# One k double of batch 3 turned by a transposing DMA instead of TensorE, in a fused sliding-window attention and MLP kernel

## The chip, the cores and the metric

The kernel runs on one core of one Trainium2 chip. The metric is the device time of one execution in microseconds (us); of several runs the median is taken. A core has five engines with a queue of instructions each: TensorE (PE, matrix products and transposes, into PSUM), VectorE (DVE), ScalarE (ACT), GpSimd (POOL) and SyncE (SP). SP computes nothing here; it issues nearly all the loads and stores and all the transposing DMAs, in the order of the program. PEld is TensorE's loading of weights, which overlaps with its products. Each engine works through its queue in order and waits for the others on semaphores.

## The reference

Eight batches of attention (8 heads, 576 tokens, head size 64) with a bias that falls linearly with distance, over a window of 128 tokens; the heads are then put side by side and go through an MLP with a hard-swish.

```python
scores = scale * np.matmul(q, k.transpose(0, 1, 3, 2))
rel = pos[:, None] - pos[None, :]
slopes = 2.0 ** (-8.0 * (np.arange(H) + 1) / H)
mask = (rel >= 0) & (rel < 128)
scores = np.where(mask, scores - slopes[:, None, None] * np.abs(rel), -1e9)
attn = softmax(scores)
x = (attn @ v).transpose(0, 2, 1, 3).reshape(B * S, H * D)     # 4608 x 512
h = x @ w_in                                                    # 4608 x 2048
out = (h * np.clip(h + 3.0, 0.0, 6.0) / 6.0) @ w_out            # 4608 x 512
```

Inputs and output are float32; inside, the kernel computes its products in bfloat16.

## The kernel before

**Groups.** Attention goes by groups g = 0 to 31: g = 4 * batch + pair of heads. A group needs q and k of its two heads turned, with the head dimension on the partitions (tiles qTb and kTb, two of each, one per parity of the batch), and v as it lies (vbuf). `scores(g)` makes the score products (lines 365 and 373), `exp_diag` and `exp_off` the exponentials on ScalarE (389, 413, 418), each followed by a mask on GpSimd (406, 415, 421), `values` the products with v (434, 442) in two parts, query tiles 0 to 2 and then 3 and 4, each followed by a reciprocal and a multiplication on VectorE into the tile avs (452, 453). `back(g)` turns avs into x^T: for g >= 8, other than 10 and 11, by a transposing DMA on SP (476); for groups 10 and 11 by five TensorE transposes and a copy on ScalarE (483, 489).

**MLP.** The tokens go in nine blocks of 512. A block has 16 up units (`moe_up`: four products at line 502, an activation on ScalarE at 521, a combination on VectorE at 522) and 16 down units (`moe_down`: four products at 552; after every fourth a VectorE copy, 561, and a store on SP, 562). These units are filler for TensorE: `fill(n)` issues the next n of them. An up unit is issued only when `done` says that all groups of its tokens have their x^T.

**Order.** The whole order of work is written by hand (a manual schedule): what the program says first goes first into each engine's queue. From batch 2 on the order is that of `segment`, whose pass g issues: scores(g); a turn, in passes 8 to 11; filler; the exponentials of g, with filler and values(g - 1) between them; back(g - 1); `stage_next(g)`; filler. In pass 12 scores(13) are issued as well, with the scores of 12 at the pass's beginning.

**How q and k get turned.** From batch 4 on, and for q of batch 3, `stage_next` loads the tokens of a whole tensor (`load_tokens`, five loads of up to 128 tokens on SP, line 112), GpSimd casts them to bfloat16 in tbuf (`cast_tokens`, 195), and one transposing DMA of 20 blocks of 128 columns turns them (`xbar`, 200). k of batch 3 goes another way: it is loaded as two doubles (four heads each; `load_double`, 98), cast by GpSimd (`prepare_double`, 228, in passes 8 and 9), and turned on TensorE by `double`: five transposes into a PSUM tile (243), a ScalarE copy to kTb (245), then four more and a second copy. Both use the PSUM buffer of tag "av", of which there is one; `values` takes its result tiles from the same buffer. The first double of k of batch 3 is turned in pass 10, the second in pass 11. Its scores come in passes 12 to 15.

**Around it on SP.** In pass 8, `stage_next` issues nothing on SP. In pass 9 SP issues x^T of group 8, then the five loads of v of batch 3 (from the table LOADS), then the transposing DMA of q of batch 3, which waits for GpSimd's five casts. v of batch 3 is cast on GpSimd in pass 12 (188, 191).

Of the kernel before, what the change touches and what calls it, by code (L numbers as in the profile page):

```python
# [11 lines left out]
BF16 = mybir.dt.bfloat16  # L12
# [6 lines left out]
def kernel(  # L19
# [9 lines left out]
    nc = tc.nc  # L29
    B, H, S, D = q.shape  # L30
# [5 lines left out]
    NP = H // 2  # L36
    NQ = 5
# [3 lines left out]
    RP, RT = 64, 9  # L41
# [24 lines left out]
    prs = ctx.enter_context(tc.tile_pool(name="prs", bufs=2))  # L66
# [14 lines left out]
    qTb = [held.tile([128, NP, NQ, 128], BF16, name=f"qTb{i}") for i in range(2)]  # L81
    kTb = [held.tile([128, NP, NQ, 128], BF16, name=f"kTb{i}") for i in range(2)]
# [19 lines left out]
    def tokens(b, nm):  # L102
        if (b, nm) not in ld:
            i = 2 + b % 2 if b < 3 else (3, 1, 0, 2)[(3 * (b - 3) + "qkv".index(nm)) % 4]
            ld[b, nm] = ldbuf[i][:, 0:NQ * H * D].rearrange("p (j h d) -> p j h d", j=NQ, h=H)
        return ld[b, nm]

    def load_tokens(b, nm):
        t = tokens(b, nm)
        for j in range(NQ):  # L110
            n = min(128, S - j * 128)
            nc.sync.dma_start(out=t[:n, j, :, :],
                              in_=src_of[nm][b, :, ds(j * 128, n), :].rearrange("h p d -> p h d"))
# [70 lines left out]
    def cast_tokens(b, nm):  # L184
        s = ld[b, nm]
        if nm == "v":
            for lo in (0, 2):
                nc.gpsimd.tensor_copy(  # L188
                    out=vbuf[b % 2][:, lo:lo + 2, :, 0:D].rearrange("p j h d -> p (j h) d"),
                    in_=s[:, lo:lo + 2, :, :].rearrange("p j h d -> p (j h) d"))  # L190
            nc.gpsimd.tensor_copy(out=vbuf[b % 2][:LAST, 4, :, 0:D], in_=s[:LAST, 4, :, :])
            return
        for j in range(NQ):
            m = min(128, S - j * 128)
            nc.gpsimd.tensor_copy(out=tbuf[:m, :, j, :],  # L195
                                  in_=s[:m, j, :, :].rearrange("p (i e) d -> p i (e d)", e=2))

    def xbar(b, nm):
        dst = (qTb if nm == "q" else kTb)[b % 2]
        nc.sync.dma_start_transpose(out=dst.rearrange("p h j c -> p (h j) c"),  # L200
                                    in_=tbuf.rearrange("p h j c -> p (h j c)"))

    st = {}
# [20 lines left out]
    def prepare_double(b, dp, copies, nms="kq", early=None):  # L224
        for nm, copy in zip(nms, copies):
            pr = prs.tile([128, RT, 2 * D], BF16, tag=f"pr{nm}", name="pr2")
            for e in range(2):
                copy(out=pr[:, :, ts(e, D)],  # L228
                     in_=ldbuf["qk".index(nm)][:, ds((2 * dp + e) * RT * D, RT * D)].rearrange(
                         "p (t d) -> p t d", t=RT))  # L230
                if early and (nm, e) == (nms[0], 0):
                    early()
            st[b, dp, nm] = pr
# [3 lines left out]
    def double(b, dp, nm, part, tag, copy):  # L237
        src = st[b, dp, nm]
        t0, t1 = ((0, 5), (5, RT))[part]
        tp = BANKS[tag].tile([128, t1 - t0, 128], BF16, tag=tag, name="tp2",  # L240
                             padded_shape=[128, 8, 128])
        for t in range(t0, t1):
            nc.tensor.transpose(tp[:, t - t0, :], src[:, t, :], ident)  # L243
        dst = (qTb if nm == "q" else kTb)[b % 2][:, 2 * dp:2 * dp + 2, :, :]
        copy(out=dst.rearrange("p i j c -> p i (j c)")[:, :, 0:S].rearrange(  # L245
                 "p i (a t) -> p i a t", t=RT)[:, :, :, t0:t1],
             in_=tp.rearrange("p t (a i) -> p i a t", i=2))

    def wide_double(b, dp, nm, copy):
# [219 lines left out]
    def by_xbar(g):  # L469
        return g >= XB and g != XB + 2 and g != XB + 3  # L470
# [103 lines left out]
    def fill(n):  # L574
        for _ in range(n):
            if at[0] == len(units):
                return
            nt, fn, step = units[at[0]]
            if fn is moe_up and done[0] < NP * (min((nt * NT + NT - 1) // S, B - 1) + 1):
                return  # L580
            fn(nt if fn is moe_up else nt - 1, step)
            at[0] += 1

    V, P, A = nc.vector.tensor_copy, nc.gpsimd.tensor_copy, nc.scalar.copy

    LOADS = {9: "v3", 10: "q4", 12: "k4", 13: "v4", 14: "q5", 16: "k5", 17: "v5", 18: "q6",
             20: "k6", 21: "v6", 22: "q7", 24: "k7", 25: "v7"}

    VCAST = {15: 4, 19: 5, 23: 6, 27: 7}
# [1 line left out]
    def stage_next(g):  # L591
        b, hp = divmod(g, NP)
        nb = b + 1
        if g == 2 * NP:
            cast_tokens(2, "v")
        for n in LOADS.get(g, "").split():
            load_tokens(int(n[1]), n[0])
        if nb == 3 and hp < 2:
            prepare_double(3, hp, (P,), "k")
        if nb == 3 and hp == 1:  # L600
            cast_tokens(3, "q")
            xbar(3, "q")
        elif nb < B and nb > 3 and hp < 2:
            cast_tokens(nb, "qk"[hp])
            xbar(nb, "qk"[hp])
        if VCAST.get(g):
            cast_tokens(VCAST[g], "v")
# [110 lines left out]
    def segment(lo, hi, fills):  # L718
        for g in range(lo, hi + 1):
            f = fills(g)  # L720
            if by_xbar(g - 2):
                done[0] = g - 1
            if lo < g < hi and g != 3 * NP + 1:
                scores(g)
            turn = {2 * NP: (2, 1, "k"), 2 * NP + 1: (2, 1, "q"),
                    2 * NP + 2: (3, 0, "k"), 2 * NP + 3: (3, 1, "k")}.get(g)
            if turn:
                double(*turn, 0, "av", A)
            fill(f[0])
            if turn:  # L730
                double(*turn, 1, *(("h", V) if turn[0] == 2 else ("av", A)))
            if g < hi:
                exp_diag(g, 0)
            fill(f[1])
            if g < hi:
                exp_diag(g, 1)
            if g == 3 * NP:
                cast_tokens(3, "v")
            if g > lo:
                values(g - 1, (0, 1, 2))  # L740
            fill(f[2])
            if g < hi:
                exp_off(g, 0)
            fill(f[3])
            if g < hi:
                exp_off(g, 1)
            if g > lo:
                values(g - 1, (3, 4))
            fill(f[4])
            if g > lo and by_xbar(g - 1):  # L750
                back(g - 1)
            fill(f[5])
            if g < hi:
                stage_next(g)
            fill(1)
            if g == 3 * NP:
                scores(g + 1)
            if g > lo and not by_xbar(g - 1):
                back(g - 1)
                done[0] = g  # L760
            fill(f[6] - 1)
# [51 lines left out]
```

## Time and profile before

| | us |
|---|---|
| median of 3 runs | 321.58 |
| the runs | 321.58, 320.84, 323.06 |
| the profiled execution | 320.94 |
| its span, first to last instruction | 319.2 |
| PE busy | 310.1 |
| PEld busy | 164.9 |
| ACT busy | 195.7 |
| DVE busy | 173.1 |
| POOL busy | 141.2 |

The profile is of one execution. Its times are counted from the first instruction. Busy times are sums of an engine's instructions, with overlaps counted once; a PE that is shown busy need not be at its peak. The granted TensorE clock was 0.999 of full speed. A row of a timeline has the start, the length, the engine, the line of the kernel, the operation, what it writes <- what it reads, shapes, how many were merged, and in brackets an idle time before it and what ended it. A `q` behind an engine's name is its queue: a row that issues a DMA. The time from the issue of a DMA to its landing stands in the table of DMA issues.

### The profile page before, as it was taken

What the parts mean: (1) busy time and instruction counts of PE and PEld (TensorE: products, weight loads), DVE (VectorE), ACT (ScalarE), POOL (GpSimd) and SP (SyncE); (2) the same over time, 40 slices, a digit from 0 to 9 for tenths busy, and PEclk for the clock granted to TensorE, in tenths of its full rate; (3) what the DMA queues carried; (4) which work ended last, traced back from release to release, by engine and by line L of the source; (5) the groups of instructions that cost most, each with busy time, mean ns of one, the idle gap of its engine ahead of it and who ended that gap; (6) DMA issues with size and microseconds to landing.
All of it is one profiled execution on the core that took longest, in us unless ns stands there. A gap on an engine that the chain in (4) does not pass through costs nothing.

```text
span 319.2 us, 7124 instructions
## 1 busy us (share of the span) xinstructions
PE 310.1 (97%) x2775; PEld 164.9 (52%) x2775; DVE 173.1 (54%) x338; ACT 195.7 (61%) x334; POOL 141.2 (44%) x249
## 2 busy tenths in 40 slices
PE   7879999999999999999999999999999999999996
PEld 5565465455545454445677654444444444444443
DVE  6667675554355655655565556555656455455510
ACT  4748976877767776676676667666764344244401
POOL 8464493684496477266744673663331000000000
PEclk9999999999999999999999999999999999999999
DMA  7999999999999999998999999962212110000112
GB/s 281 199 323 225 256 260 195 249 231 194 215 252 157 239 208 211 205 222 194 207 205 211 209 190 196 225 93 68 38 39 88 53 36 33 33 33 35 66 56 75
DMA packets 131425, 51.90 MB, mean 163 GB/s; under 512 B 118976, under 2 KB 123328, under 8 KB 131392
## 3 DMA queue, kind: packets, MB, share of 16 engines
q1 hardware_dynamic: 126160, 45.36, 68.0%
q0 software_dynamic: 4224, 4.19, 8.2%
q10 hardware_dynamic: 1008, 1.90, 1.6%
q8 instruction: 21, 0.34, 0.5%
q14 instruction: 12, 0.10, 0.1%
HBM read 36.70 MB, written 9.44 MB: 145 GB/s over the span
## 4 chain that ended last, share of the span: by engine, by line
PE 86%; DMA 5%; ACT 4%; POOL 2%; DVE 2%; issue 1%; POOLq 0%
PE ops L552 38%; PE hps L502 36%; DMA w_in_sb<-in_moe_w_in_dram 3%; PE sce L365 3%; PE av L442 2%; PE av L434 2%; DMA ldbuf<-in_k_dram 2%; ACT r L521 2%; PE ops L533 1%; ACT kTb L245 1%; ACT gbuf L399 1%; PE tp L243 1%; DVE gbuf L522 0%; ACT gbuf L377 0%; PE tb L483 0%
## 5 line engine op out<-in xcount | busy, mean ns | idle before, releaser
L522 DVE SCALAR_TENSOR_TENSOR gbuf<-r,hps 128x512 bf16<-128x512 f32 x144 | 98.7, 688 | 101.0 <-ACT r L521 99.8
L521 ACT ACTIVATE r<-hps,bias 128x512 f32<-128x512 f32 x144 | 98.9, 689 | 86.8 <-PE hps L502 86.6
L502 PE MATMUL hps<-xT,w_in_sb 128*128 128x512 bf16 (+1 forms) x640 | 144.9, 358 | 0.6 <-ACT xT L489 0.3
L552 PE MATMUL ops<-w_out_sb,gbuf 128*128 128x512 bf16 x560 | 137.8, 379 | 0.0
L502 PEld LDWEIGHTS <-w_in_sb 128*128 128x128 bf16 x640 | 59.3, 98 | 55.0 <-issue 0.8
L552 PEld LDWEIGHTS <-gbuf 128*128 128x128 bf16 x560 | 51.9, 98 | 56.3
L415 POOL TENSOR_SCALAR_AFFINE_SELECT po<-po 128x512 bf16<-128x512 bf16 x48 | 30.3, 636 | 32.5 <-ACT po L413 32.4
L406 POOL TENSOR_SCALAR_AFFINE_SELECT pd<-pd 128x512 bf16<-128x512 bf16 x48 | 29.8, 634 | 33.5 <-ACT pd L389 33.5
L389 ACT ACTIVATE pd<-sce,bias_d 128x512 bf16<-128x512 f32 x48 | 31.7, 684 | 5.4 <-PE sce L373 2.7
L561 DVE COPY osb<-ops 128x512 f32<-128x512 f32 x33 | 22.7, 688 | 20.0 <-PE ops L552 17.5
L195 POOL CAST tbuf<-ldbuf 128x512 bf16<-128x512 f32 (+1 forms) x45 | 25.6, 614 | 16.8 <-issue 9.3
L413 ACT ACTIVATE po<-sce,bias_o 128x512 bf16<-128x512 f32 x48 | 33.0, 687 | 0.0
L453 DVE TENSOR_TENSOR avs<-av,rc 128x384 bf16<-128x384 f32 (+1 forms) x48 | 23.6, 491 | 1.6
L442 PEld LDWEIGHTS <-pd 128*128 128x128 bf16 x192 | 14.3, 97 | 8.3 <-issue 0.5
L434 PE MATMUL av<-vbuf,po 128*128 128x65 bf16 x192 | 18.0, 193 | 0.0
L442 PE MATMUL av<-vbuf,pd 128*128 128x65 bf16 x192 | 17.3, 193 | 0.3 <-ACT kTb L245 0.3
L434 PEld LDWEIGHTS <-po 128*128 128x128 bf16 x192 | 14.3, 98 | 2.9 <-DVE avs L453 0.5
L188 POOL CAST vbuf<-ldbuf 128x1024 bf16<-128x1024 f32 x14 | 14.2, 1043 | 3.5 <-DMA ldbuf<-in_v_dram 3.5
L418 ACT ACTIVATE p4buf<-sce,bias_d 128x64 bf16<-128x64 f32 x48 | 15.5, 323 | 0.0
L228 POOL CAST pr<-ldbuf 128x576 bf16<-128x576 f32 x20 | 12.9, 670 | 5.1 <-DMA ldbuf<-in_k_dram 3.1
L365 PE MATMUL sce<-qTb,kTb 64*64 64x192 bf16 (+1 forms) x368 | 11.9, 245 | 0.0
L365 PEld LDWEIGHTS <-kTb 64*64 64x64 bf16 x368 | 7.1, 106 | 8.6 <-issue 8.5
(104 smaller groups left out, 208.4 us busy)
## 6 DMA issues: line engine op xcount, KB each, us to landing
out_dram<-osb SPq DMA_DIRECT2D x33, 256.0 KB, 2.5
ldbuf<-in_v_dram SPq DMA_DIRECT2D x32, 256.0 KB, 5.2
ldbuf<-in_q_dram SPq DMA_DIRECT2D x20, 256.0 KB, 5.3
ldbuf<-in_k_dram SPq DMA_DIRECT2D x16, 256.0 KB, 4.4
ldbuf<-in_q_dram SPq DMA_DIRECT2D x12, 288.0 KB, 7.0
ldbuf<-in_k_dram SPq DMA_DIRECT2D x12, 288.0 KB, 6.3
w_in_sb<-in_moe_w_in_dram POOLq DMA_DIRECT2D x4, 512.0 KB, 9.2
w_out_sb<-in_moe_w_out_dram POOLq DMA_DIRECT2D x4, 512.0 KB, 10.3
```

The lines of the kernel that those rows point to most:

```text
L195: nc.gpsimd.tensor_copy(out=tbuf[:m, :, j, :], in_=s[:m, j, :, :].rearrange("p (i e) d -> p i (e d)", e=2))
L365: nc.tensor.matmul(sce[e][lo:lo + 64, j, :, :].rearrange("p s c -> p (s c)")[:, ds(lo, n)], lhsT=kT[r, j, lo:lo + 64], rhs=qT[r, ds(128 * ...
L389: nc.scalar.activation(out=pd[:, e, :, :], in_=st["sce"][e][:, :, 0, :], func=ACT.Exp, bias=bias_d[:, h:h + 1], scale=scale)
L406: nc.gpsimd.affine_select(out=pd[:, e, :, :], in_=pd[:, e, :, :], pattern=[[0, 4], [1, 128]], channel_multiplier=-1, base=0, compare_op=AL ...
L413: nc.scalar.activation(out=po[:, e, :, :], in_=sc[:, :, 1, :], func=ACT.Exp, bias=bias_o[:, h:h + 1], scale=scale)
L415: nc.gpsimd.affine_select(out=po[:, e, :, :], in_=po[:, e, :, :], pattern=[[0, 4], [-1, 128]], channel_multiplier=1, base=-1, compare_op=A ...
L434: nc.tensor.matmul(out_av, lhsT=po[:, e, qt % 4 if full(g) else qt - 1, :], rhs=vb[:, qt - 1, h, :], start=True, stop=False)
L442: nc.tensor.matmul(out_av, lhsT=d, rhs=vb[:, qt, h, :], start=(qt == 0), stop=True)
L502: nc.tensor.matmul(hps[:, lo:hi], lhsT=w_in_sb[:, ks, ts(ms, 128)], rhs=xT[:, ks, ds(src, hi - lo)], start=(ks == 0), stop=(ks == n_ks - 1))
L521: nc.scalar.activation(out=r6, in_=hps, func=ACT.Relu, bias=bias3[:, 0:1], scale=1.0 / 6.0)
L522: nc.vector.scalar_tensor_tensor(out=gts[nt][:, ms, :], in0=r6, scalar=1.0, in1=hps, op0=ALU.min, op1=ALU.mult)
L552: nc.tensor.matmul(ops[nt, sub], lhsT=gts[nt][:, ms, ts(sub, 128)], rhs=w_out_sb[:, ms, :], start=(ms == 0), stop=(ms == n_ms - 1))
```

## The change

Three things change, all for batch 3.

- k's first double is no longer turned on TensorE in pass 10. Right after GpSimd's cast of it, in pass 8, SP issues a transposing DMA of its nine blocks of 128 columns into a tile of the pool `prs` (tag "prq", whose two buffers held the q doubles of batch 2). In SP's queue it stands behind a store and ahead of x^T of group 8. In pass 11, between the two parts of values(10), VectorE copies the whole double from that tile to kTb. Nine TensorE transposes and two ScalarE copies are gone; one DMA and one VectorE copy of 128x1152 are new. The copy writes what the two ScalarE copies wrote, and the scores of groups 12 and 13 read it.
- The second double is turned as before, in pass 11.
- v's five loads of batch 3 are no longer issued together by the table. Two blocks are loaded in pass 9, where the five stood, then comes q's transposing DMA, and then the other three blocks.

Nothing else in the order of any engine's queue is changed.

```diff
-    def load_tokens(b, nm):
+    def load_tokens(b, nm, blocks=range(NQ)):
         t = tokens(b, nm)
-        for j in range(NQ):
+        for j in blocks:
...
+    def turn_double(b, dp, nm):
+        src = st.pop((b, dp, nm))
+        tp = st[b, dp, nm] = prs.tile([128, RT, 2 * D], BF16, tag="prq", name="pt2")
+        nc.sync.dma_start_transpose(out=tp, in_=src.rearrange("p t c -> p (t c)"))
+
+    def copy_double(b, dp, nm, copy):
+        tp = st.pop((b, dp, nm))
+        dst = (qTb if nm == "q" else kTb)[b % 2][:, 2 * dp:2 * dp + 2, :, :]
+        copy(out=dst.rearrange("p i j c -> p i (j c)")[:, :, 0:S].rearrange(
+                 "p i (a t) -> p i a t", t=RT),
+             in_=tp.rearrange("p t (a i) -> p i a t", i=2))
...
-    LOADS = {9: "v3", 10: "q4", 12: "k4", 13: "v4", 14: "q5", 16: "k5", 17: "v5", 18: "q6",
+    LOADS = {10: "q4", 12: "k4", 13: "v4", 14: "q5", 16: "k5", 17: "v5", 18: "q6",
...
         if nb == 3 and hp < 2:
             prepare_double(3, hp, (P,), "k")
+        if nb == 3 and hp == 0:
+            turn_double(3, 0, "k")
         if nb == 3 and hp == 1:
+            load_tokens(3, "v", range(0, 2))
             cast_tokens(3, "q")
             xbar(3, "q")
+            load_tokens(3, "v", range(2, NQ))
...
-                    2 * NP + 2: (3, 0, "k"), 2 * NP + 3: (3, 1, "k")}.get(g)
+                    2 * NP + 3: (3, 1, "k")}.get(g)
...
             if g > lo:
                 values(g - 1, (0, 1, 2))
             fill(f[2])
+            if g == 2 * NP + 3:
+                copy_double(3, 0, "k", V)
             if g < hi:
                 exp_off(g, 0)
```

## The prediction

> **What bounds the kernel now.** The page comes first: span, busy time of each engine, shares of the chain that ended last.
>
> ```profile
> span 319.2 us, 7124 instructions
> ...
> PE 310.1 (97%) x2775; PEld 164.9 (52%) x2775; DVE 173.1 (54%) x338; ACT 195.7 (61%) x334; POOL 141.2 (44%) x249
> ...
> PE 86%; DMA 5%; ACT 4%; POOL 2%; DVE 2%; issue 1%; POOLq 0%
> ```
>
> TensorE (PE) is busy for 97% of the span and makes 86% of the chain. VectorE (DVE), ScalarE (ACT) and GpSimd (POOL) are idle for 39% to 56% of it. So time is saved only where PE gets less to do, or waits less, and work given to another engine is free until PE has to wait for it.
>
> The second view is the chain of waits around the removed work, in the pass g = 10 of the segment loop (start, length, what; all in us):
>
> ```profile
> 68.86 0.43 PE sce L365 x14
> 69.29 0.05 PE sce L373 x4
> 69.34 0.39 PE tp L243 x5
> 69.73 0.88 PE hps L502 x4
> 70.61 0.02 issue
> 70.63 0.39 ACT r L521
> 71.02 0.19 issue
> 71.22 0.73 ACT kTb L245
> 71.95 0.04 issue
> 71.99 0.22 PE av L442 x2
> ```
>
> The reader is to see two things. The five transposes stand on the chain themselves (0.39). And the chain leaves PE afterwards: the attention matmuls (av) want the one PSUM buffer of tag "av", in which the turned k still lies until ScalarE has copied it out (0.73); that copy itself stood behind an activation (L521).
>
> **What the removed part is worth.** I measure it against stages without a turn. The third view gives busy time in three stretches, each from the first score matmul of a pass to its first av matmul: g = 10, then 14 and 15. Columns: stretch, length, busy time and count of PE, PEld, DVE, ACT and POOL, granted clock, DMA share, GB/s.
>
> ```profile
> 68.80:71.99 3.19, 3.02 (x38) 1.69 (x38) 1.89 (x3) 2.12 (x4) 3.19 (x7) 1.00 1.13 249
> 98.16:100.38 2.22, 2.22 (x30) 1.19 (x30) 1.45 (x3) 1.27 (x2) 0.47 (x3) 1.00 1.09 243
> 105.33:107.55 2.22, 2.22 (x30) 1.19 (x30) 0.79 (x2) 1.27 (x2) 1.01 (x3) 1.00 1.30 223
> ```
>
> All three hold the same other work: one set of scores, one unit of four up matmuls and one of four down matmuls. Both plain stages take 2.22, the one with the turn 3.19, at the same clock (1.00). The nine transposes with the wait behind them therefore cost 3.19 - 2.22 = 0.97. The chain gives nearly the same: 71.99 - 69.34 = 2.65, less 0.88 of up matmuls and as much for the down matmuls beside the ACT pieces, leaves 0.89. I take 0.97. The turn of the second double in pass 11 stays as it was, with its wait.
>
> ScalarE loses two copies (one is the 0.73 above), which brings nothing more: in this pass its later work follows PE's matmuls and moves with them.
>
> **What is added on VectorE.** One copy of 128x1152, put behind the first half of values in pass 11, ahead of the second half. No row shows this copy from SBUF. The nearest are copies of the same shape and stride from PSUM; then VectorE, PE and POOL where the new one will stand, in the times of before:
>
> ```profile
> L257 DVE COPY qTb<-tp 128x1152 bf16<-128x1152 bf16 x2 | 2.7, 1355 | 0.3 <-PE tp L255 0.3
> ```
>
> ```profile
> 82.07 0.56 DVE L453 TENSOR_TENSOR avs<-av,rc 128x384 bf16<-128x384 f32 x1
> 83.47 0.18 DVE L452 RECIPROCAL rc<-av 128x4 f32<-128x4 f32 x1 [0.84 <-PE av L442]
> 83.69 0.42 DVE L453 TENSOR_TENSOR avs<-av,rc 128x256 bf16<-128x256 f32 x1
> ```
>
> ```profile
> 84.99 0.44 PE L483 MATMUL tb<-ident,avs 128*128 128x128 bf16 x5
> 85.37 0.52 PE L365 MATMUL sce<-qTb,kTb 64*64 64x192 bf16 x16
> ```
>
> ```profile
> 82.45 1.41 POOL L415 TENSOR_SCALAR_AFFINE_SELECT po<-po 128x512 bf16<-128x512 bf16 x2
> 83.81 0.29 POOL L421 TENSOR_SCALAR_AFFINE_SELECT p4buf<-p4buf 128x128 bf16<-128x128 bf16 x1
> ```
>
> VectorE is free at 82.07 + 0.56 = 82.63 and waits 0.84 for PE. Behind the copy are queued the second reciprocal, the second avs and an osb copy; avs is awaited by PE's transposes (L483). Those begin at 84.99, avs ends at 83.69 + 0.42 = 84.11. The room is 0.84 + (84.99 - 84.11) = 1.72. At 1.36 the copy lies in it with 0.36 to spare; a faster copy, down to nothing, changes nothing. Beyond 1.72 each us costs a us. Its other reader, the scores of batch 3 (L365), stands at 85.37, later than L483. All these rows follow PE and move 0.97 earlier together.
>
> [...]
>
> **What is added and moved on SP.** SP is the one queue for loads, transposing DMAs and most stores. It gets a transpose of nine 128-blocks before x^T of group 8; the transpose of q (batch 3) passes three of v's five loads.
>
> ```profile
> 69.05 1.35 SPq L476 DMA_TRANSPOSE xT<-avs  x1
> 70.46 5.51 SPq L112 DMA_DIRECT2D ldbuf<-in_v_dram  x5
> 76.08 3.81 SPq L200 DMA_TRANSPOSE qTb<-tbuf  x1
> ...
> 82.20 4.50 SPq L112 DMA_DIRECT2D ldbuf<-in_q_dram  x5
> ```
>
> ```profile
> SPq L562 <- DVE rc L452: 1.8, 1, 1.8
> ```
>
> Five blocks took 1.35 to issue, twenty 3.81: 0.164 a block and 0.53 besides, so nine cost 2.0. That is the worst by which everything behind slips. The other end is a gain: 5.51 for five loads of v is over the 4.50 for q's, and with the transpose between them the loads have more time to drain; I do not count on it. SP waits 1.8 for VectorE's third store in pass 12 (the second fence: SP's waits between 60 and 95); with PE 0.97 earlier that room is 0.8 to 0.9. Who waits for what is queued behind:
>
> ```profile
> ldbuf<-in_v_dram SPq DMA_DIRECT2D x1, 128.0 KB, 5.4
> ```
>
> ```profile
> 89.92 0.61 POOL L191 CAST vbuf<-ldbuf 64x512 bf16<-64x512 f32 x1
> ...
> 91.91 2.84 POOL L195 CAST tbuf<-ldbuf 128x512 bf16<-128x512 f32 x5
> ```
>
> - *v's last block* is issued by 70.46 + 5.51 = 75.97 and, at 5.4 from issue to landing (third fence), is there by 81.4. At worst it comes 3.81 + 2.0 later, 87.2; POOL's cast of it stands at 89.92 - 0.97 = 88.95. Hidden by 1.7.
> - *q of batch 4*: its fifth load begins a fifth of 4.50, 0.9, before 86.70 and with the same 5.4 lands at 91.2; 2.0 later is 93.2. POOL casts it as the last fifth of 91.91 to 94.75, from 94.2 - 0.97 = 93.2. At worst it is just in time.
> - *q of batch 3* comes earlier unless both bounds fall badly; *x^T* of group 8 (69.05) is first read once group 11 is done, behind 85.37.
> - *k of batch 4* is the tightest:
>
> ```profile
> 105.82 3.83 SPq L200 DMA_TRANSPOSE kTb<-tbuf  x1
> ```
>
> ```profile
> kTb<-tbuf SPq DMA_TRANSPOSE x1, 5.4
> ```
>
> ```profile
> 112.50 0.52 PE L365 MATMUL sce<-qTb,kTb 64*64 64x192 bf16 x16
> ```
>
> Issued at 105.82 and 5.4 to landing, it is there at 111.2; the scores that read it stood at 112.50 and now come at 111.53. The margin shrinks from 1.3 to 0.3 if SP keeps its old times. The worst slip of 2.0 less the wait of 1.8 leaves 0.2 on SP's old times, so even that fits. I take zero for SP, with this margin as the weak point.
>
> The new wait on SP costs nothing: the transpose wants POOL's two casts of k, done at 63.32 + 1.28 = 64.60, while SP is busy with what stands ahead of it until 69.05.
>
> ```profile
> 63.32 1.28 POOL L228 CAST pr<-ldbuf 128x576 bf16<-128x576 f32 x2
> ```
>
> **Sum.** -0.97 + 0 + 0. The span becomes 319.2 - 0.97 = 318.2. The profiled execution took 320.94, 1.7 more than its span, and would take 319.97. The median of the runs is 321.58, 0.64 over the profiled one, so the median becomes 320.61; I say 320.6.
>
> **Rivals.**
>
> *1. Only part comes back.* The stall behind the turn could be covering something else, such as the av matmuls' own operands, and only the transposes go: 0.39 for five, so 0.70 for nine. Against it: the plain stages show 2.22 twice, without any wait. Time 321.58 - 0.70 = 320.9. Chance 0.10.
>
> *2. The VectorE copy comes too late.* POOL's masks lie at 82.45 to 84.10 (83.81 + 0.29), just where the copy starts. If it must wait for all of them, it runs from 84.10 to 85.46, the second half of avs follows (83.47 to 84.11, 0.64) and ends at 86.10, 1.11 after PE wants it: the gain is gone, 321.7. It decides once the copy with its delay takes over 1.72. [...] Against: one mask is 0.7 long, and if the copy waits for only one, both together are 2.06, 0.34 over, which leaves 0.63 of the gain, 320.95. Chance 0.08.
>
> *3. Slower: the transposing of k of batch 4 comes late.* DMA share is at or above 1 in all three stretches above, so the transfers have no idle time to give. If SP's slip of 2.0 is kept instead of being absorbed at the store, k lands at 113.2 and PE waits at its scores until then: 113.2 - 112.50 = 0.7 later than before, 322.3. It eats the gain from a slip of 0.3 on and makes the kernel slower from 1.3 on. Against it: SP's wait of 1.8 and the loads' 5.51, of which up to 1.0 (against 4.50) can come back. Chance 0.12; a slip that grows from batch to batch and passes 1% takes 0.03 of it.
>
> **Numbers.** The forecast keeps 0.68. A measurement of this kernel tells 1% (3.2) from no change; none of the cases but that last 0.03 reaches it, and 0.02 is left for a gain over 1% that none of these rows shows. So: faster 0.02, same 0.95, slower 0.03. The three runs of before lie 2.2 apart (320.84 to 323.06); half of that, 1.1, on the forecast gives 319.5 to 321.7, which holds rivals 1 and 2; the upper end goes to 322.6 to take in rival 3.
>
> **What would show it.** In the new profile: no L243 in pass 10; the stretch from first score to first av matmul there 2.2; pass 11 still 3.2; a VectorE copy from SBUF of at most 1.4 before the reciprocal of pass 11, and PE's L483 right behind its down matmuls; no wait of PE before the scores of batch 4. The forecast is wrong if PE idles before L483 of pass 11 or before the scores of group 16, or if SP's third store of pass 12 goes out later than VectorE allows.

## The result, and the profile after

The changed kernel takes 323.98 us (median of 22 runs, 321.63 to 325.82); the kernel before, run beside it, 322.15 (22 runs, 320.54 to 324.59). The ratio is 1.006, 95% interval 1.0042 to 1.0078: about 1.8 us slower, where 1.0 faster was forecast, and above the range.

The profiled execution took 323.19, its span is 321.4. The page of the changed kernel, span and busy time:

```profile
span 321.4 us, 7066 instructions
...
PE 306.6 (95%) x2727; PEld 164.9 (51%) x2766; DVE 175.1 (54%) x339; ACT 194.3 (60%) x332; POOL 141.0 (44%) x249
```

Before had 2775 matmuls and the change takes away nine; 2727 shows that some records are missing here, so busy PE is not compared, and the reading goes by the starts of PE's products. New functions push the line numbers up: PE's score products are L377 here and were L365, values' products L446 and L454 (L434, L442), down products L564 (L552).

The gain is there. Busy time of the changed kernel from the first score matmul of pass 10 to its first av matmul, then from scores(15) to scores(16) (columns as in the prediction):

```profile
69.79:72.01 2.22, 2.17 (x29) 1.19 (x30) 1.25 (x2) 0.67 (x2) 2.22 (x5) 1.00 1.22 243
...
105.33:114.76 9.43, 7.70 (x67) 3.69 (x67) 4.72 (x10) 5.47 (x10) 7.07 (x13) 1.00 1.20 231
```

Pass 10 now takes 2.22 like the plain stages, 0.97 less. The second row is where it is lost. The same stage before, in the same view:

```profile
105.33:112.50 7.17, 7.17 (x68) 3.58 (x68) 4.53 (x10) 5.45 (x10) 2.77 (x6) 1.00 1.20 230
```

PE was busy without a gap there; now the stage is 2.26 longer, with GpSimd busy for 7.07 instead of 2.77. The profiled runs add up: this execution of the changed kernel reached pass 10 at 69.79, 0.99 later than before's (68.80; nothing that the change touches comes earlier), gained 0.97, lost 2.26, and from there to the end stays 2.2 to 2.3 later: 321.4 against 319.2.

What PE waits for, from the timeline of the changed kernel's PE:

```profile
108.16 0.20 PE L454 MATMUL av<-vbuf,pd 128*128 128x65 bf16 x1 [0.45 <-POOL pd L418]
108.75 0.20 PE L454 MATMUL av<-vbuf,pd 128*128 128x65 bf16 x1 [0.38 <-POOL pd L418]
109.33 0.20 PE L446 MATMUL av<-vbuf,po 128*128 128x65 bf16 x1 [0.38 <-POOL po L427]
...
109.92 0.20 PE L446 MATMUL av<-vbuf,po 128*128 128x65 bf16 x1 [0.35 <-POOL po L427]
...
110.11 1.03 PE L564 MATMUL ops<-w_out_sb,gbuf 128*128 128x512 bf16 x4
110.97 1.89 PE L514 MATMUL hps<-xT,w_in_sb 128*128 128x512 bf16 x8
...
114.76 0.52 PE L377 MATMUL sce<-qTb,kTb 64*64 64x192 bf16 x16
```

These are the products of values(14), and each waits for one of the four masks of group 14, which GpSimd hands over one at a time. Why the masks are late, from GpSimd's timeline, first before, then after:

```profile
100.27 2.84 POOL L195 CAST tbuf<-ldbuf 128x512 bf16<-128x512 f32 x5 [1.75 <-DMA qTb<-tbuf]
103.06 1.22 POOL L406 TENSOR_SCALAR_AFFINE_SELECT pd<-pd 128x512 bf16<-128x512 bf16 x2
```

```profile
104.68 2.83 POOL L195 CAST tbuf<-ldbuf 128x512 bf16<-128x512 f32 x5 [6.17 <-issue]
107.47 1.21 POOL L418 TENSOR_SCALAR_AFFINE_SELECT pd<-pd 128x512 bf16<-128x512 bf16 x2
108.65 1.21 POOL L427 TENSOR_SCALAR_AFFINE_SELECT po<-po 128x512 bf16<-128x512 bf16 x2
```

Ahead of the masks in GpSimd's queue stand the five casts of k of batch 4 into tbuf. There is one tbuf for q and k, so they wait until the transposing DMA of q of batch 4 has read it. The row of before names that wait (1.75, behind the DMA qTb<-tbuf); in the row of after the idle time has grown to 6.17, and its cause is not inferred ("issue"), but its end fits: the DMA lands at about 104.5 (below), and the casts begin at 104.68.

Why q's DMA is late, from SP's timeline, before and after:

```profile
68.39 0.56 SPq L562 DMA_DIRECT2D out_dram<-osb  x1
...
86.80 3.20 SPq L562 DMA_DIRECT2D out_dram<-osb  x3
90.06 4.50 SPq L112 DMA_DIRECT2D ldbuf<-in_k_dram  x5
94.77 3.85 SPq L200 DMA_TRANSPOSE qTb<-tbuf  x1
```

```profile
69.34 0.57 SPq L574 DMA_DIRECT2D out_dram<-osb  x1
...
72.13 1.22 SPq L488 DMA_TRANSPOSE xT<-avs  x1
...
82.93 1.25 SPq L488 DMA_TRANSPOSE xT<-avs  x1
84.25 6.10 SPq L112 DMA_DIRECT2D ldbuf<-in_q_dram  x5
90.45 1.52 SPq L574 DMA_DIRECT2D out_dram<-osb  x3
92.03 5.44 SPq L112 DMA_DIRECT2D ldbuf<-in_k_dram  x5
97.64 3.86 SPq L200 DMA_TRANSPOSE qTb<-tbuf  x1
```

The store ahead of the new transpose is issued at 69.34 instead of 68.39: 0.95 of the lateness below is this execution's late start. The new transpose puts x^T of group 8 2.13 further back (72.13 against 69.05). By x^T of pass 11, 82.93 against 80.88, 1.03 of it is made good. But then q's five loads take 6.10 to issue instead of 4.50, so the three stores begin 3.65 later. They give back 1.68 (1.52 instead of 3.20; that is the wait for VectorE). k's loads start 1.97 later and take 5.44 instead of 4.50, so q's transposing DMA is issued 2.87 later, 1.92 of it without the late start. And it needs longer to land, by the tables of DMA issues, after, before, and in a second profiled execution of the kernel before (run g1 below):

```profile
qTb<-tbuf SPq DMA_TRANSPOSE x1, 6.9
```

```profile
qTb<-tbuf SPq DMA_TRANSPOSE x1, 5.3
```

```profile
qTb<-tbuf SPq DMA_TRANSPOSE x1, 7.3
```

So it lands at about 104.5 instead of 100.1, GpSimd's casts begin 4.41 later, and what is left of that at PE is 2.26. The longer landing is not the change's doing. In the four other profiled executions without an added DMA (g1, e5, f3, f4) the same DMA took 7.1 to 7.6, and in the eleven with an added DMA 6.6 to 7.5; the 5.3 of before's first profile, on which the prediction was worked out, is the exception. Of the 4.41, then, 0.95 is the late start, 1.92 is SP's slip, and some 1.5 is that one quick landing. PE reaches scores(15) at 105.33 in both, because its late start and its gain of 0.97 cancel there; what SP keeps of the late start is, seen from PE, the gain.

### The profile page after: what moved, and what is told of

Its sections match the earlier page's. It is cut to its first block, busy times and chain, and to the rows that moved or that the text cites. A ratio compares the mean times of both kernels' runs of the same rounds, so it can differ in the third digit from the quotient of the medians.

```text
span 321.4 us, 7066 instructions
## 1 busy us (share of the span) xinstructions
PE 306.6 (95%) x2727; PEld 164.9 (51%) x2766; DVE 175.1 (54%) x339; ACT 194.3 (60%) x332; POOL 141.0 (44%) x249
## 4 chain that ended last, share of the span: by engine, by line
PE 64%; issue 3%; POOL 1%; DMA 0%; DVE 0%; POOLq 0%
PE ops L564 30%; PE hps L514 27%; PE sce L377 2%; PE av L454 2%; PE av L446 1%; PE ops L545 1%; POOL tbuf L195 1%; POOL pd L418 0%; POOL po L427 0%; DMA qTb<-tbuf 0%; PE sce L385 0%; DVE osb L548 0%; POOLq L195 0%; POOLq L427 0%
## 5 line engine op out<-in xcount | busy, mean ns | idle before, releaser
L514 PE MATMUL hps<-xT,w_in_sb 128*128 128x512 bf16 (+1 forms) x622 | 142.8, 357 | 2.4 <-DMA w_in_sb<-in_moe_w_in_dram 0.8
L564 PE MATMUL ops<-w_out_sb,gbuf 128*128 128x512 bf16 x539 | 133.8, 379 | 3.0 <-issue 2.1
L564 PEld LDWEIGHTS <-gbuf 128*128 128x128 bf16 x560 | 51.9, 98 | 57.1 <-issue 0.7
L454 PEld LDWEIGHTS <-pd 128*128 128x128 bf16 x192 | 14.4, 97 | 9.2 <-POOL pd L418 1.4
L446 PE MATMUL av<-vbuf,po 128*128 128x65 bf16 x192 | 18.1, 193 | 0.8 <-POOL po L427 0.7
L454 PE MATMUL av<-vbuf,pd 128*128 128x65 bf16 x192 | 17.8, 194 | 1.0 <-POOL pd L418 0.8
L446 PEld LDWEIGHTS <-po 128*128 128x128 bf16 x192 | 14.3, 98 | 3.9 <-POOL po L427 1.0
L377 PE MATMUL sce<-qTb,kTb 64*64 64x192 bf16 (+1 forms) x368 | 11.9, 245 | 0.0
L377 PEld LDWEIGHTS <-kTb 64*64 64x64 bf16 x368 | 7.1, 106 | 8.6 <-issue 8.5
```

Of the source, the lines that this page charges most:

```text
L377: nc.tensor.matmul(sce[e][lo:lo + 64, j, :, :].rearrange("p s c -> p (s c)")[:, ds(lo, n)], lhsT=kT[r, j, lo:lo + 64], rhs=qT[r, ds(128 * ...
L446: nc.tensor.matmul(out_av, lhsT=po[:, e, qt % 4 if full(g) else qt - 1, :], rhs=vb[:, qt - 1, h, :], start=True, stop=False)
L454: nc.tensor.matmul(out_av, lhsT=d, rhs=vb[:, qt, h, :], start=(qt == 0), stop=True)
L514: nc.tensor.matmul(hps[:, lo:hi], lhsT=w_in_sb[:, ks, ts(ms, 128)], rhs=xT[:, ks, ds(src, hi - lo)], start=(ks == 0), stop=(ks == n_ks - 1))
L564: nc.tensor.matmul(ops[nt, sub], lhsT=gts[nt][:, ms, ts(sub, 128)], rhs=w_out_sb[:, ms, :], start=(ms == 0), stop=(ms == n_ms - 1))
```

## The experiments

The table lists them all (us); each has the runs of the kernel before on the same chip beside it. The last row's are single runs.

| run | what it is | median | before beside it | ratio, 95% interval |
|---|---|---|---|---|
| e5_v_split_alone | before, v loaded by two and three | 322.16 | 322.29 | 0.9998, 0.9978 to 1.0018 |
| e4_v_in_one | changed, v's loads together | 324.20 | 322.29 | 1.0054, 1.0028 to 1.0081 |
| e3_dma_alone | before and the new DMA, unread | 323.71 | 322.29 | 1.0043, 1.0011 to 1.0076 |
| h1_plain_copy_alone | before and a plain DMA of the same bytes, unread | 323.48 | 322.52 | 1.0034, 1.0005 to 1.0062 |
| f1_less_v | changed, two of v's loads left out | 321.54 | 322.36 | 0.9979, 0.9955 to 1.0003 |
| f4_second_half_h | before, second halves of the turns into "h" | 321.97 | 322.36 | 0.9996, 0.9971 to 1.0021 |
| f3_before_two_tbufs | before, one tbuf each for q and k | 322.02 | 322.36 | 0.9991, 0.9968 to 1.0013 |
| e1_two_tbufs | changed, one tbuf each | 323.21 | 322.29 | 1.0021, 0.9995 to 1.0046 |
| f2_two_tbufs_v4_split | e1, v of batch 4 by two and three | 322.99 | 322.36 | 1.0026, 1.0001 to 1.0051 |
| h2_two_tbufs_v4_three_two | e1, v of batch 4 by three and two | 322.06 | 322.52 | 0.9987, 0.9964 to 1.0011 |
| g1, g2, g3, g4 (again) | before, changed, e1, f2: a second profile of each | 323.24, 324.13, 322.65, 322.31 | 321.56 | none |

### Which part costs: v's order, the DMA's issue, or its transfer

**v's order alone.** The kernel before with only this, and the changed kernel without it:

```diff
-    LOADS = {9: "v3", 10: "q4",
+    LOADS = {10: "q4",
...
+            load_tokens(3, "v", range(0, 2))
             cast_tokens(3, "q")
             xbar(3, "q")
+            load_tokens(3, "v", range(2, NQ))
```

> The kernel before with only v's loads of batch 3 split, two ahead of q's transposing DMA and three behind it; k turned on TensorE as before. Theory A: ratio 1.000, within 0.2%. Theory B: 1.006 or more, with the same wait for GpSimd's masks. Theory C: 1.000.

Measured 0.9998.

```diff
-            load_tokens(3, "v", range(0, 2))
+            load_tokens(3, "v")
             cast_tokens(3, "q")
             xbar(3, "q")
-            load_tokens(3, "v", range(2, NQ))
```

> The changed kernel with v's five loads of batch 3 issued together ahead of q's transposing DMA, as before. Theory A: about as slow as the changed kernel, ratio 1.004 to 1.007. Theory B: the loss is gone, ratio 0.997. Theory C: 1.006.

Measured 1.0054, as slow as the changed kernel. The order of v's loads is not the cause, in either direction.

**The DMA alone.** The kernel before, with the new transpose issued in pass 8 into the same tile, which nobody reads; the turn on TensorE stays:

```diff
+    def turn_unread(b, dp, nm):
+        tp = prs.tile([128, RT, 2 * D], BF16, tag="prq", name="pt2")
+        nc.sync.dma_start_transpose(out=tp, in_=st[b, dp, nm].rearrange("p t c -> p (t c)"))
...
             prepare_double(3, hp, (P,), "k")
+        if nb == 3 and hp == 0:
+            turn_unread(3, 0, "k")
```

> The kernel before, with the transposing DMA of k's first double added on SP and its result left unread; TensorE, ScalarE and VectorE as before. Theory A: the full price without the gain, 2.3 to 2.9 us, ratio 1.007 to 1.009, with TensorE waiting for GpSimd's masks in the first half of values(14). Theory B and theory C: ratio 1.000.

Measured 1.0043, 1.4 us: the DMA by itself makes the kernel before slower, less than expected. VectorE's new copy isn't in this run, so the loss doesn't need it. Its profile has the changed kernel's wait at the same place, in PE's waits between 100 and 130 (columns: who waits for whom, sum, times, longest):

```profile
PE av L438 <- POOL po L419: 0.7, 2, 0.4
```

**The same bytes without transposing.** The same kernel with a plain DMA from SBUF to SBUF in its place:

```diff
-        nc.sync.dma_start_transpose(out=tp, in_=st[b, dp, nm].rearrange("p t c -> p (t c)"))
+        nc.sync.dma_start(out=tp, in_=st[b, dp, nm])
```

> The kernel before with a plain DMA of the same 128x1152 elements (288 KB, from SBUF to SBUF, result unread) in the place of the transposing DMA of the run with the DMA alone, which measured 1.004. SP issues a plain one in about 0.6 us where the transpose took 2. If it is SP's time that the added DMA costs (1.4 us more of it), this run is at 1.000 to 1.002 and q of batch 4 is turned at most 1 us later than before. If it is the transfer (about 1 us of all queues), it is at 1.003 to 1.005 as the transpose.

SP's timeline of this run, then of the changed kernel:

```profile
70.30 0.53 SPq L251 DMA_DIRECT2D pt<-pr  x1
```

```profile
70.01 2.02 SPq L252 DMA_TRANSPOSE pt<-pr  x1
```

The plain one occupies SP for 0.53 instead of 2.02, yet the kernel is at 1.0034, not far from 1.0043 with the transpose. By the median, then, a slowdown is there without SP's long issue. But the two signs that were named disagree: the time is the one named for the transfer, while q of batch 4 is sent to be turned only 0.8 us later, as named for SP's time. This is counted from the store ahead of the added DMA (68.39 in before): q's transposing DMA goes out after 26.4 to 27.0 us in the five profiles without an added DMA, after 27.1 with the plain one, and after 27.6 to 28.4 in the nine with the transposing one and all of v's loads. In the stage where the loss arises, h1's profile lost 0.51 and e3's 1.29 (table below). With intervals as wide as these (0.2 to 2.0 us for h1, 0.4 to 2.4 for e3), how the cost divides between SP's issue and the transfer stays open. The 1 us named for the transfer was an estimate: 288 KB at the 223 to 249 GB/s of the prediction's three stretches take 1.2 to 1.3 us. The transposing DMA of the changed kernel landed 4.3 us after its issue. What both runs have is that the loads behind the added DMA take longer to issue: five loads of q or k of batch 4 took 4.29 to 5.04 in the five profiles without it, and 5.24 to 6.10 in the ten with it and all of v's loads (5.39 and 5.42 in h1).

**Less to transfer.** The changed kernel without the loads of blocks 2 and 3 of v of batch 3:

```diff
-            load_tokens(3, "v", range(2, NQ))
+            load_tokens(3, "v", range(4, NQ))
```

> The changed kernel without two of the five loads of v of batch 3 (blocks 2 and 3 are left out, 2 x 256 KB, and the old contents of the buffer are used in their place), so that SP and the transfers carry about what they did before, or less. Theory A (the added transfer fills a path of loads and transposes that had no room left): q of batch 4 is turned as early as before, TensorE waits neither for GpSimd's masks in pass 15 nor for k of batch 4 in front of the scores of group 16, and the whole gain shows, ratio 0.997. Theory C (VectorE copy and GpSimd's masks): the loss stays, 1.006. Theory D (the transposing DMA disturbs later ones by its kind, not by its share of the queue): the loss stays, 1.004 to 1.006.

Measured 0.9979: with two loads fewer on the queue the loss is gone and the median stands 0.8 below before's, though the interval just reaches 1. Two loads fewer are also less for SP to issue, so this run doesn't tell issue and transfer apart either.

### One line through all profiles

If the chain read above is the cause, PE's loss must follow from one thing alone: when GpSimd can begin the casts of k of batch 4, seen from scores(15). All profiled runs with one tbuf, in order (us; start of the casts less start of scores(15); start of the down products behind the first part of values(14) less start of scores(15); what that is over before's 2.52):

| run | casts | down products | lost |
|---|---|---|---|
| before | -5.06 | 2.52 | 0 |
| e5_v_split_alone | -3.23 | 2.51 | 0 |
| f4_second_half_h | -2.86 | 2.57 | 0.05 |
| g1_before_again | -2.60 | 2.82 | 0.30 |
| f1_less_v | -2.58 | 2.84 | 0.32 |
| h1_plain_copy_alone | -2.39 | 3.03 | 0.51 |
| e3_dma_alone | -1.62 | 3.81 | 1.29 |
| e4_v_in_one | -0.81 | 4.61 | 2.09 |
| changed kernel | -0.65 | 4.78 | 2.26 |
| g2_after_again | -0.15 | 5.28 | 2.76 |

Every loss is the casts' start plus 2.91 (2.26 + 0.65 of the changed kernel), to within 0.01, and nothing below -2.91. The kernel before had 2.15 to spare in its profiled execution (5.06 - 2.91), e5 had 0.32, f4 nothing, and neither had another execution of the very same kernel:

> A second profile of the kernel before, because the first, at 320.94 us, is among its quickest of 22 runs (320.54 to 324.59, median 322.15) and executions differ by 0 to 2.9 us in how late TensorE reaches the scores of group 10, ahead of all that the change touches. Expected: a later start than in the first profile, and the same distance from the scores of group 10 to the end, that is no wait of TensorE around group 15; the theory of a late queue says that the kernel before has enough room for a start some 1 us late.

Its GpSimd timeline and, for the late start of that execution, one of PE's waits before 70:

```profile
104.72 2.83 POOL L195 CAST tbuf<-ldbuf 128x512 bf16<-128x512 f32 x5 [4.22 <-DMA qTb<-tbuf]
```

```profile
PE tp L255 <- POOL pr L228: 1.9, 1, 1.9
```

Here the releaser is named again: 4.22 behind the DMA of q. This execution started pass 10 at 70.80, 2.0 later than the first, and lost 0.30 in the stage that the first went through unharmed.

The table shows one thing more. e3, which has the DMA and not the gain, lost 1.29; the changed kernel lost 2.26, 0.97 more. Counted from scores(10), the casts begin after 34.89 in both, and PE reaches scores(15) after 36.51 in e3 and after 35.54 in the changed kernel. It comes 0.97 sooner and waits that much longer: the gain isn't kept beside the loss, it goes into the wait. That both have the same 34.89 is luck (35.40 in g2, 34.74 in e4); that the casts don't come sooner with PE shows in all three.

### Taking GpSimd's wait away

The changed kernel with a tbuf of its own for q and for k, so that k's casts don't wait for q's DMA:

```diff
-    tbuf = held.tile([128, NP, NQ, 128], BF16, name="tbuf")
+    tbufs = {nm: held.tile([128, NP, NQ, 128], BF16, name=f"tbuf{nm}") for nm in "qk"}
...
-            nc.gpsimd.tensor_copy(out=tbuf[:m, :, j, :],
+            nc.gpsimd.tensor_copy(out=tbufs[nm][:m, :, j, :],
...
-                                    in_=tbuf.rearrange("p h j c -> p (h j c)"))
+                                    in_=tbufs[nm].rearrange("p h j c -> p (h j c)"))
```

> The changed kernel with two buffers tbuf, one for q and one for k, so that GpSimd's cast of k of batch 4 no longer waits until q's transposing DMA has landed. Theory A (the queue on SP slips, q of batch 4 is turned over 4 us late, GpSimd stands before its cast of k and the masks of group 14 behind it keep TensorE waiting for 2.3 us): that wait is gone, only the gain of 0.97 is left, ratio to the kernel before 0.997, and the scores of group 16 begin about 1 us earlier than before's 112.5 less whatever the start of the run differs. Theory B (it is the new order of v's loads, not the added DMA): the same here. Theory C (the VectorE copy and GpSimd's masks shut each other out): nothing changes, ratio 1.006.

Measured 1.0021: better than the changed kernel's 1.006 (the intervals overlap by a little), but the gain did not come. The waits behind masks are gone; another took their place, in PE's waits between 100 and 130 of this run and of its second profile:

> A second profile of the changed kernel with two buffers tbuf, whose median (ratio 1.002) is worse than its first profile says (0.36 us gained from group 10 on). Theory A with the second limit (k of batch 4 landing behind the scores of group 16): a later start and a longer wait for k of batch 4 there, 1 to 2 us in place of 0.62. If the start alone is late and the wait is 0.6 again, the median is owed to the first 60 us.

```profile
PE sce L377 <- DMA kTb<-tbufk: 0.5, 1, 0.5
```

```profile
PE sce L377 <- DMA kTb<-tbufk: 1.2, 1, 1.2
```

Now scores(16) wait for the transposing DMA of k of batch 4, which stands in SP's queue behind all five loads of v of batch 4. That is the place of the prediction's third rival; in the changed kernel it is hidden, because PE is late already.

The control is the kernel before with the same two buffers:

> The kernel before with two buffers tbuf alone, as a control for the runs above: GpSimd waits there for q's transpose in the kernel before too (1.75 us at the cast of k of batch 4), but TensorE does not wait for the masks behind it. Theory A: 1.000, at most 0.3% faster where a late start of a run makes TensorE wait after all.

Measured 0.9991: nothing that this run can tell from zero is won by them in the kernel before, so what they bring to the changed kernel is the return of a loss.

**Both limits.** In the next one, v of batch 4 is split around k's transposing DMA, two blocks ahead of it and three behind:

```diff
-             12: "k4", 13: "v4", 14: "q5"
+             12: "k4", 14: "q5"
...
         elif nb < B and nb > 3 and hp < 2:
+            if (nb, hp) == (4, 1):
+                load_tokens(4, "v", range(0, 2))
             cast_tokens(nb, "qk"[hp])
             xbar(nb, "qk"[hp])
+            if (nb, hp) == (4, 1):
+                load_tokens(4, "v", range(2, NQ))
```

> As the run with two buffers tbuf, and v of batch 4 loaded by two and three blocks as well, so that k of batch 4 is turned three loads earlier. In the run with two buffers alone TensorE waited 0.5 us for k of batch 4 and 0.62 of the 1.0 gained was gone at the scores of group 16. Theory A with this second wait: the wait is gone, ratio 0.996 to 0.998 in place of 1.002. If something else made that run's median, it stays at 1.002.

Measured 1.0026. The first profile has no wait from scores(15) to scores(16) (7.17), but that execution had started 2.9 later than before's; the second profile shows a third limit:

> A second profile of the kernel with two buffers tbuf and v of batch 4 split, whose median (1.0026) is worse than its first profile says (0.72 us gained from group 10 on, after a start 2.9 us late). Expected: again no wait of TensorE at groups 14 to 16, 0.7 gained from group 10 on, whatever the start.

```profile
PE av L446 <- DVE avs L465: 1.1, 1, 1.1
```

From pass 10 to the end this execution took 0.65 more than before's first, not 0.7 less. The wait is in pass 16, at the second part of values(15). Behind it is again a DMA; VectorE's timeline of the same run:

```profile
118.05 0.56 DVE L465 TENSOR_TENSOR avs<-av,rc 128x384 bf16<-128x384 f32 x1 [1.86 <-DMA xT<-avs]
```

VectorE may not write avs until the transposing DMA to x^T has read that buffer; it was issued at 112.14, behind the last three loads of v, and took 5.8 to land. The next run has the split the other way round, three blocks ahead and two behind:

```diff
-                load_tokens(4, "v", range(0, 2))
+                load_tokens(4, "v", range(0, 3))
...
-                load_tokens(4, "v", range(2, NQ))
+                load_tokens(4, "v", range(3, NQ))
```

> The changed kernel with two buffers tbuf and v of batch 4 loaded by three and two blocks around k's transposing DMA, so that neither GpSimd's cast, nor k, nor v of batch 4 should be late. If these three are all that takes the gain away: no wait of TensorE from group 14 to 18 and 0.9 gained from group 10 on, ratio 0.997 to 0.999. If the path of loads and transposes simply has no room left for the added one: some other wait appears there, ratio 1.000 to 1.003.

GpSimd's timeline in this run:

```profile
97.30 1.73 POOL L195 CAST tbufk<-ldbuf 128x512 bf16<-128x512 f32 x3
99.37 1.17 POOL L195 CAST tbufk<-ldbuf 128x512 bf16<-128x512 f32 x2 [0.34 <-DMA ldbuf<-in_k_dram]
100.50 1.22 POOL L418 TENSOR_SCALAR_AFFINE_SELECT pd<-pd 128x512 bf16<-128x512 bf16 x2
```

The casts wait only for their loads, the masks follow at 100.50, scores(15) to scores(16) take 7.16 (104.17 to 111.33), and VectorE waits for no x^T behind them; the same DMA landed 3.5 after its issue. Whether the split or chance brought that, one profile doesn't tell. The span is 318.1, 1.1 under before's, from 0.2 earlier at pass 10: the gain is kept in this execution. In time it is 0.9987, with an interval (0.9964 to 1.0011) wholly below the changed kernel's (1.0042 to 1.0078). That it is faster than the kernel before is not shown.

### Another way to the same gain

The stall in pass 10 came from the second half of the turned double occupying the "av" buffer. This leaves the turn on TensorE, adds no DMA, and puts the second half in the buffer "h", copied by VectorE, in passes 10 and 11:

```diff
-                           *(("h", V) if turn[0] == 2 else ("av", A)))
+                           "h", V)
```

> The kernel before, where the second half of both doubles of k of batch 3 is turned into a PSUM buffer of tag h and copied by VectorE, as those of batch 2 are, in place of tag av and ScalarE. Nothing is added on SP. In pass 9, which is written so, the stretch from the scores to the first attention product is 2.72 us against 3.19 in passes 10 and 11. If the wait for the one av buffer is what the turn costs beside its nine transposes, both passes fall to 2.7, the span by 0.9, ratio 0.997. If the h buffer or VectorE is then late for the up units, 1.000 or above.

Measured 0.9996. Pass 10 from first score to first av matmul takes 2.72 instead of 3.19, but in pass 11 the up products now wait for that buffer (PE's timeline):

```profile
81.07 1.02 PE L502 MATMUL hps<-xT,w_in_sb 128*128 128x512 bf16 x4 [1.28 <-DVE gbuf L522]
```

### A second cost on top of the wait

> A second profile of the changed kernel. Theory A: the gain of 0.97 in pass 10 again, and again a loss of 2 to 3 us in the first half of values(14), by GpSimd's cast of k of batch 4 behind q's transposing DMA; the later the start of the run, the larger.

The second profile of the changed kernel lost 4.44 between scores(15) and scores(16), of which the table above explains 2.76. The rest is behind the masks, where PE waits for nothing. Its timeline of PE, and windows of busy time with the granted clock in the third column from the end:

```profile
109.39 1.17 PE L564 MATMUL ops<-w_out_sb,gbuf 128*128 128x512 bf16 x4
110.34 3.48 PE L514 MATMUL hps<-xT,w_in_sb 128*128 128x512 bf16 x8
...
115.72 0.52 PE L377 MATMUL sce<-qTb,kTb 64*64 64x192 bf16 x16
```

```profile
106.75:110.17 3.42, 1.62 (x14) 0.89 (x15) 1.24 (x3) 1.82 (x4) 3.42 (x8) 1.00 1.37 214
110.17:113.45 3.28, 3.28 (x10) 1.17 (x8) 1.33 (x3) 0.69 (x1) 0.98 (x2) 0.50 1.04 261
```

The eight up products that take 1.89 in the first profile take 3.48 here, at a granted clock of 0.50. From the end of the wait to scores(16) it is 115.72 - 109.39 = 6.33, against 112.50 - 107.85 = 4.65 before: 1.68 more, and 2.76 + 1.68 = 4.44. The profile of e4_v_in_one has the same (3.41 us at 0.50), and 10.94 instead of 7.17 for the stage.

The mean clock that each run lists tells how often: 0.993 to 0.995 (half the clock for 3.4 of some 322 us makes 0.995) in 6 of the changed kernel's 22 runs, 7 of 12 of e4, 3 of 12 of e3; 1 in 36 of the three kernels on the changed one with two tbufs (e1, f2, h2); 2 of 12 of f1, none of h1's 12, 2 in 36 of e5, f3 and f4; 6 in 93 of the runs of the kernel before beside the experiments. The six runs of the changed kernel have a median of 325.1, the other sixteen 323.2. Where in a run without a trace the clock fell isn't shown.

## Why the prediction was wrong

- **The gain in pass 10, 0.97: right.** The stretch went from 3.19 to 2.22. Rival 1 (0.70 only) falls.
- **The VectorE copy, 1.36 in a room of 1.72: right in what came of it, the copy a little longer.** The timeline of the changed kernel around it:

```profile
82.45 2.15 POOL L427 TENSOR_SCALAR_AFFINE_SELECT po<-po 128x512 bf16<-128x512 bf16 x2
...
82.55 1.55 DVE L257 COPY kTb<-pt 128x1152 bf16<-128x1152 bf16 x1
...
84.22 0.43 DVE L465 TENSOR_TENSOR avs<-av,rc 128x256 bf16<-128x256 f32 x1
...
85.00 0.44 PE L495 MATMUL tb<-ident,avs 128*128 128x128 bf16 x5
85.37 0.52 PE L377 MATMUL sce<-qTb,kTb 64*64 64x192 bf16 x16
```

  The copy took 1.55, more than the 1.4 named as its most; avs ends at 84.65 and PE wants it at 85.00, which leaves 0.35 where 0.36 was forecast. Of rival 2 this much is there: the two masks that ran beside the copy took 2.15 instead of 1.41, and so in all nine profiles with the copy and none of the seven without it. That the copy must wait for the masks was the author's estimate from where their rows lie, and it did not: it began 0.10 behind the first of the two and ran beside them. Why the masks took 0.74 longer is not shown. Here it was GpSimd that paid, and it had the time: its next mask begins at 86.78 in both profiles, after 1.94 idle instead of 2.68.
- **SP at zero: the step that failed.** The issue time, 2.0, was right (2.02; x^T of group 8 goes out 2.13 later, counted from the store ahead). Three things about it were not.
  - It was to be absorbed by the 1.8 that SP waits at the third store of pass 12, leaving 0.2. The wait did give back 1.68, and 1.03 was made good ahead of it, but the loads on both sides of it took 1.60 and 0.94 longer to issue. So 1.92 was left at q's transposing DMA, not 0.2. The loads' issue was taken to have up to 1.0 to give back; it took 2.54 more.
  - The list of who waits for what is queued behind had the casts of q and k of batch 4 as waiting for their loads, and k's DMA as the tightest. It left out that k's casts also wait for q's DMA, because both go through one tbuf, and that the masks of group 14 are queued behind those casts. Before's GpSimd timeline has this wait (1.75 at 100.27). The room there was 2.15 in that execution (5.06 - 2.91), and 4.41 was taken: 4.41 - 2.15 = 2.26.
  - All times and rooms were read from one execution of the kernel before, in which q's DMA happened to land in 5.3. The other profiles without an added DMA and with one tbuf had 0.32 of room or none. With no room, SP's slip and the gain of 0.97 both go into the wait.
- **Rival 3 (322.3): the right cause, one step too late and too small.** It said that the transfers have no idle time to give and that SP's slip of 2.0 would be kept; 1.92 was. It put the wait at scores(16), for k's DMA, at 0.7; it came a stage earlier, at the masks of group 14, with 2.26 in the profiled run. The wait at scores(16) exists too, and shows once the first is removed (e1: 0.5, g3: 1.2).
- **The sum.** With the measured terms the first profiled run gives -0.97 + 2.26 = +1.3. In g2 the fall of the clock adds 1.68. The sixteen runs with a mean clock of 0.999 or 1.000 have a median of 323.2, 1.1 above before's; all 22 stand 1.8 above. Of the distance from the forecast's 320.6 to 323.98, 0.57 is the baseline: three runs of before had a median of 321.58, the 22 have 322.15.
- **The signs that were named.** It was to be wrong if PE idled before L483 of pass 11 or before the scores of group 16, or if SP's third store of pass 12 went out later than VectorE allows. The first two did not happen: PE idled in values(14), a place that the prediction had not watched. The third did. VectorE has that store's data ready at 89.65, by its timeline after:

```profile
88.96 0.69 DVE L573 COPY osb<-ops 128x512 f32<-128x512 f32 x1
```

  SP begins the three stores only at 90.45 and issues them in 1.52, without a wait. The wait of 1.8 was used up, and SP was late from there on.

What stays open: how the cost divides between SP's issue and the transfer; why a transposing DMA of 20 blocks needs 5.3 us to land in one execution and 7.3 in another of the same kernel (g1); and why executions reach pass 10 up to 3.1 us apart. e3's loss was smaller than expected and the medians of e1 and f2 worse than their first profiles; late starts and a larger wait at the second limit are seen in single profiles, but they are not shown to make up the difference. Issuing the new DMA from another engine's queue was not tried.

## What to carry to other kernels

Before a DMA is added to a loaded queue, follow the next transfers to the engines that wait for them, through shared buffers too (who may not write until the DMA has read?), and on to what is queued behind the waiting instruction. Here q of batch 4 landed at about 100.1 in before's first profile, 12.4 ahead of its own reader (scores(16), at 112.50), but the room through the shared tbuf was 2.15. Don't count an added transfer by its issue time alone: here, with a DMA share of 1.09 to 1.30 in the prediction's three stretches, five loads behind it took 5.24 to 6.10 to issue instead of 4.29 to 5.04. A gain ahead of a place that already waits for a DMA can go into that wait, as the 0.97 did here. A room that one profile shows should be checked in a second execution, since here the same kernel had 2.15 us to spare in one and none in the other.

## What the runs showed of the hardware that was not expected

- In two profiles a wait of PE was followed by a second cost. In g2 PE was busy for 1.62 of the 3.42 us up to 110.17, and then ran for 3.28 us at a granted clock of 0.50: 2.76 went into the wait and 1.68 behind it. In e4 it was busy for 2.01 of 3.42, and then came 3.41 us at 0.50. In the first profile of the changed kernel it was busy for 1.84 of 3.41, less than in e4, and the clock stayed at 1.00; its window of busy time:

```profile
106.80:110.21 3.41, 1.84 (x16) 0.79 (x14) 0.74 (x2) 2.05 (x4) 3.41 (x8) 1.00 1.29 217
```

  So how little PE did does not by itself tell whether the clock falls. What decides it is not shown.
- A plain DMA from SBUF to SBUF and a transposing one of the same 128x1152 can't be told apart by what they cost the kernel (1.0034, 1.0005 to 1.0062, and 1.0043, 1.0011 to 1.0076), though SP needs 0.53 us for the one and 2.02 for the other.
- The issue of five loads of the same size (q or k of batch 4) took from 4.29 to 6.10 us on SP: 4.29 to 5.04 without the added DMA, 5.24 to 6.10 behind it, and 4.84 and 5.27 in f1, where two loads of v are left out. So the issue time of a load is no constant here.
